# Linear attention and a GELU MLP on one core: loads in order of use, a reordered layer norm, masks between layer norms, x reloaded, z as a bf16 pair

## Chip, cores, metric

One core of one Trainium2 chip. The metric is the device time of one execution in microseconds (us). The changed kernel and the kernel before run on the same chip in turn, several times each. TensorE multiplies matrices into banks of its result memory, PSUM; VectorE, ScalarE and GpSimd work elementwise; each has its own queue of instructions, in program order. All runs compared below are of the fast state, or single looks (state unknown), which are called so. The span in the profile is just under 2 us shorter than the device time.

## The reference

```python
def _layernorm(x): return (x - mean(x)) / sqrt(var(x) + 1e-5)        # over the last axis
# attention, H = 32 heads of 20:
q, k, v = split(xn @ wqkv)
phi = lambda t: where(t > 0, t + 1, exp(t)) + 1e-6
kv  = einsum("bhsd,bhse->bhde", phi(k), v)
z   = einsum("bhsd->bhd", phi(k))
o   = einsum("bhqd,bhde->bhqe", phi(q), kv) / (einsum("bhqd,bhd->bhq", phi(q), z) + 1e-6)
A   = o @ wo
B   = gelu(xn @ w1 + b1) @ w2 + b2
out = x + A + B            # xn = _layernorm(x); x: 1 x 2048 x 640, F = 1536, all bf16
```

The kernel never forms v. It takes G = xnᵀ·phi(k), then KV from Wv and G, then M = KV·Wo, so that the attention's output is phi(q)/den · M, and it accumulates this in the same PSUM banks as the MLP's second product. S = 2048 gives 16 token tiles of 128.

## The kernel before

A small planner records instructions per engine in program order and puts in semaphore waits from declared reads and writes. TensorE's order is: warm-up fillers, MLP first product (with a transpose of the next tile between its units), K, G ("KV" below), Q chunk 0, z, KV, Q chunk 1, M, den, Q chunks 2 and 3, output tiles. The parts that the change touches (cuts marked; lines that are only comments sum up what is cut):

```python
        x_res = sb("x_res", [P, NT, D], BF16)          # x, kept for the residual
        xn_tm = sb("xn_tm", [P, NT, D], BF16)          # normalised x
        xnT = sb("xnT", [P, DT, S], BF16)              # its transpose
        PKQ = sb("PKQ", [P, NT * D], BF16)             # phi(k), later phi(q)
        # ... cut ...
        dma_x(0, 1)
        for i in range(NW1 - 1):
            dma_w1("scalar", i)                        # W1 quarters 0..2 in ScalarE's queue
        # b1, then
        dma_x(1, 1); dma_x(2, 2)
        dma_w1("sync", NW1 - 1)
        # x4..15, Wk, Wq, Wv, b2, Wo, W2 in SyncE's queue
        # ... cut ...
        def ln_stats(t):
            s = t % 4
            xt = x_res[:, t, :]
            Pl.ins(v, lambda e: e.bn_stats(stats[:, s, 0:6], xt[:, 0:HW]),
                   reads=[r_x[t]], writes=[r_stats[s]])
            ev = Pl.ins(v, lambda e: e.bn_stats(stats[:, s, 6:12], xt[:, HW:D]),
                        reads=[r_x[t]], writes=[r_stats[s]])
            Pl.ins(v, lambda e: e.bn_aggr(aggr[:, s, :], stats[:, s, :]),
                   reads=[r_stats[s]], writes=[r_aggr[s]])
            # ... cut: GpSimd computes rstd from aggr ...
        def ln_norm(t):
            s = t % 4
            Pl.ins(v, lambda e: e.tensor_scalar(xn_tm[:, t, :], x_res[:, t, :], aggr[:, s, 0:1], rstd[:, s:s + 1],
                                                ALU.subtract, ALU.mult),
                   reads=[r_x[t], r_aggr[s], r_rstd[s]], writes=[r_xn[t]])
        # ... cut: transp(t), five TensorE transposes, then VectorE's copy to xnT ...
        # ... cut ...
        filler(11)
        ln_stats(0)
        ln_stats(1)            # waits for x1 ...
        ln_norm(0)             # ... and this stands behind it
        b1_step()
        transp(0)
        filler(2)
        ln_stats(2)
        ln_norm(1)
        segs = [(0, 1), (1, 1), (2, 1), (3, 1), (4, 2), (6, 2), (8, 4), (12, 4)]
        for (t0, n) in segs:
            for jb in range(JT):                       # 12 units of 128 MLP columns
                while ...:                             # a next transpose is due
                    transp(nxt); ln_stats(nxt + 2); ln_norm(nxt + 1)
                h_unit(t0, n, jb)
        const_masks()                                  # GpSimd, after all layer norms
        # ... cut ...
        def phi(src, b, nb, dst, res_dst, extra_w):
            # ... cut: et, e2, d2, br; ek has three buffers ...
            Pl.ins("scalar", lambda e: e.activation(e2, src, ACT.Exp), reads=br, writes=[r_ek[s]])
            Pl.ins(v, lambda e: e.tensor_scalar(et, et, 1.0, 1e-6, ALU.min, ALU.add),      # "the min/add"
                   reads=[r_ek[s]], writes=[r_ek[s]])
            Pl.ins(v, lambda e: e.scalar_tensor_tensor(out=d2, in0=src, scalar=0.0, in1=e2,
                                                       op0=ALU.max, op1=ALU.add),
                   reads=br + [r_ek[s]], writes=[res_dst] + extra_w)
        # ... cut ...
        def z_step():
            b = take(1)
            Pl.ins("tensor", [(lambda e, j=j: e.matmul(bank(b, 2 * j, 2 * j + 1), zsum[:, j:D:DT], onesf[:],
                                                       start=True, stop=True)) for j in range(DT)],
                   reads=[r_zsum, r_small], writes=[B_[b]])
            # ... cut ...
        def den_step(c):
            # TensorE: den; VectorE: + 1e-6, reciprocal -> rden,
            # VectorE: five times PQ = PQ * rden       "the PQ multiplies"
        def xb(t):             # on GpSimd: "the additions"
            Pl.ins(g, lambda e: e.tensor_tensor(out=x_res[:, t, :], in0=x_res[:, t, :], in1=b2bc[:], op=ALU.add),
                   reads=[r_x[t], r_b2], writes=[r_x[t]])

        for t in range(NT):
            xb(t)              # as soon as GpSimd has finished the masks
        q_chunk(0); z_step(); kvt_step(); q_chunk(1); m_step(); den_step(0)
        q_chunk(2); q_chunk(3)
        # output tiles: 24 matmuls HG x W2 and 10 PQ x M into one bank pair,
        # VectorE: out_sb = PSUM + x_res, SyncE: store
```

Of the kernel before, what the change touches and what calls it, by code (L numbers as in the profile page):

```python
# [5 lines left out]
ALU = AluOpType  # L6
ACT = mybir.ActivationFunctionType
P = 128
# [104 lines left out]
def bass_parallel_sum__linear_attn_block__dense_activation_gelu__prompt_kernel(  # L113
# [23 lines left out]
    with contextlib.ExitStack() as es:  # L137
        sb = lambda *a, **k: es.enter_context(nc.sbuf_tensor(*a, **k))

        x_res = sb("x_res", [P, NT, D], BF16)  # L140
        xn_tm = sb("xn_tm", [P, NT, D], BF16)
        xnT = sb("xnT", [P, DT, S], BF16)
        PKQ = sb("PKQ", [P, NT * D], BF16)
        PK = PKQ[:].rearrange("p (t d) -> p t d", t=NT)
        PQ = PKQ[:].rearrange("p (j s) -> p j s", j=DT)
# [8 lines left out]
        Msb = sb("Msb", [P, DT, D], BF16)  # L154
# [7 lines left out]
        onesf = sb("onesf", [P, 1], FP32)  # L162
# [6 lines left out]
        zsum = sb("zsum", [P, D], FP32)  # L169
# [27 lines left out]
        r_x = [R_("x%d" % t) for t in range(NT)]  # L197
        r_xb = [R_("xb%d" % t) for t in range(NT)]
# [18 lines left out]
        r_zsum, r_z, r_ZB = R_("zsum"), R_("z"), R_("ZB")  # L217
# [6 lines left out]
        def dma_x(t, n):  # L224
            src = xv[t * P:(t + n) * P, :].rearrange("(t p) d -> p t d", p=P)
            Pl.ins("sync", lambda e: e.dma_start(x_res[:, t:t + n, :], src),
                   writes=r_x[t:t + n], dma=True)
# [6 lines left out]
        FW = F // NW1  # L234
        dma_x(0, 1)
        def dma_w1(eng, i):
            dma_w(eng, W1[:, :, i * FW:(i + 1) * FW], w1v[:, :, i * FW:(i + 1) * FW], r_W1[i])
        for i in range(NW1 - 1):
            dma_w1("scalar", i)
        dma_w("sync", b1tmp[:], B_b1.rearrange("(a p) -> a p", p=P), r_b1tmp)  # L240
        dma_x(1, 1)
        dma_x(2, 2)
        dma_w1("sync", NW1 - 1)
# [13 lines left out]
        Pl.ins(g, lambda e: e.memset(onesf[:], 1.0), writes=[r_small])  # L257
# [6 lines left out]
        def const_masks():  # L264
            def band(dst, res, base, n, step):
                Pl.ins(g, lambda e: e.memset(dst, 1.0), writes=[res])
                Pl.ins(g, lambda e: e.affine_select(
                    out=dst, in_=dst, compare_op=ALU.is_ge, fill=0.0,
                    base=base, pattern=[[-step, n], [0, step]], channel_multiplier=1),
                    reads=[res], writes=[res])  # L270
                Pl.ins(g, lambda e: e.affine_select(
                    out=dst, in_=dst, compare_op=ALU.is_ge, fill=0.0,
                    base=step - 1 - base, pattern=[[step, n], [0, step]], channel_multiplier=-1),
                    reads=[res], writes=[res])
            for t in range(DT):
                band(maskKV[t][:], r_masks, P * t - e0[t], Wd[t] // DH, DH)
            band(bmask[:], r_bmask, 0, H, 4)
# [15 lines left out]
        def ln_stats(t):  # L293
            s = t % 4
            xt = x_res[:, t, :]
            Pl.ins(v, lambda e: e.bn_stats(stats[:, s, 0:6], xt[:, 0:HW]),  # L296
                   reads=[r_x[t]], writes=[r_stats[s]])
            ev = Pl.ins(v, lambda e: e.bn_stats(stats[:, s, 6:12], xt[:, HW:D]),  # L298
                        reads=[r_x[t]], writes=[r_stats[s]])
            Pl.ins(v, lambda e: e.bn_aggr(aggr[:, s, :], stats[:, s, :]),  # L300
                   reads=[r_stats[s]], writes=[r_aggr[s]])
            Pl.ins(g, lambda e: e.tensor_single_scalar(veps[:, s:s + 1], aggr[:, s, 1:2], EPS, ALU.add),
                   reads=[r_aggr[s]], writes=[r_veps[s]])
            Pl.ins(g, lambda e: e.tensor_tensor(out=rstd[:, s:s + 1], in0=veps[:, s:s + 1],
                                                in1=mhalf[:], op=ALU.pow),
                   reads=[r_veps[s], r_small], writes=[r_rstd[s]])

        def ln_norm(t):
            s = t % 4
            Pl.ins(v, lambda e: e.tensor_scalar(xn_tm[:, t, :], x_res[:, t, :], aggr[:, s, 0:1], rstd[:, s:s + 1],  # L310
                                                ALU.subtract, ALU.mult),
                   reads=[r_x[t], r_aggr[s], r_rstd[s]], writes=[r_xn[t]])

        def transp(t):
            b = take(1)
            pT = bank(b).bitcast(BF16)[:, 0:D]
            Pl.ins("tensor", [(lambda e, k=k: e.transpose(pT[:, k * P:(k + 1) * P],  # L317
                                                          xn_tm[:, t, k * P:(k + 1) * P], ident[:]))
                              for k in range(DT)],
                   reads=[r_xn[t], r_ident], writes=[B_[b]])  # L320
            Pl.ins(v, lambda e: e.tensor_copy(xnT[:, :, t * P:(t + 1) * P],  # L321
                                              pT.rearrange("p (k q) -> p k q", k=DT)),
                   reads=[B_[b]], writes=[r_xnT[t]])
# [12 lines left out]

        filler(11)
        ln_stats(0)
        ln_stats(1)
        ln_norm(0)  # L340
        b1_step()
        transp(0)
        filler(2)
        ln_stats(2)
        ln_norm(1)
        segs = [(0, 1), (1, 1), (2, 1), (3, 1), (4, 2), (6, 2), (8, 4), (12, 4)]
        now, nxt = 0.0, 1
        for (t0, n) in segs:
            for jb in range(JT):
                while nxt < NT and (nxt < t0 + n or now >= 1.9 + 2.45 * (nxt - 1)):  # L350
                    transp(nxt)
                    if nxt + 2 < NT:
                        ln_stats(nxt + 2)
                    if nxt + 1 < NT:
                        ln_norm(nxt + 1)
                    nxt += 1
                    now += 0.3
                h_unit(t0, n, jb)
                now += 0.285 * n
        const_masks()  # L360
# [18 lines left out]
        for t in range(NT):  # L379
            b = take(2)  # L380
            fns = []
            for k in range(DT):
                for h in range(2):
                    fns.append(lambda e, k=k, h=h, b=b, t=t: e.matmul(  # L384
                        bank(b + h, 0, HW), xnT[:, k, t * P:(t + 1) * P],
                        Wqkv[:, k, D + h * HW:D + (h + 1) * HW], start=(k == 0), stop=(k == DT - 1)))
            Pl.ins("tensor", fns, reads=[r_xnT[t], r_Wk], writes=B_[b:b + 2])
            phi(pair(b), b, 2, PK[:, t, :], r_PK[t], [])
# [13 lines left out]
        Pl.ins(v, lambda e: e.tensor_tensor(out=zsum[:], in0=PK[:, 0, :], in1=PK[:, 1, :], op=ALU.add),  # L402
               reads=[r_PK[0], r_PK[1]], writes=[r_zsum])
        for t in range(2, NT):
            Pl.ins(v, lambda e, t=t: e.tensor_tensor(out=zsum[:], in0=zsum[:], in1=PK[:, t, :], op=ALU.add),  # L405
                   reads=[r_PK[t], r_zsum], writes=[r_zsum])


        def q_chunk(c):
            cc = slice(c * CW, (c + 1) * CW)  # L410
            for j in range(DT):
                b = take(1)
                Pl.ins("tensor", [(lambda e, k=k, j=j, b=b: e.matmul(  # L413
                    bank(b), Wqkv[:, k, j:D:DT], xnT[:, k, cc],
                    start=(k == 0), stop=(k == DT - 1))) for k in range(DT)],
                    reads=[r_Wq] + r_xnT[c * CH:(c + 1) * CH], writes=[B_[b]])
                phi(bank(b), b, 1, PQ[:, j, cc], r_PQ[c][j], r_PK)

        def z_step():
            b = take(1)  # L420
            Pl.ins("tensor", [(lambda e, j=j: e.matmul(bank(b, 2 * j, 2 * j + 1), zsum[:, j:D:DT], onesf[:],  # L421
                                                       start=True, stop=True)) for j in range(DT)],
                   reads=[r_zsum, r_small], writes=[B_[b]])
            Pl.ins(v, lambda e: e.tensor_copy(z_sb[:], bank(b, 0, 2 * DT)[:, 0:2 * DT:2]), reads=[B_[b]], writes=[r_z])
            for j in range(DT):
                Pl.ins(v, lambda e, j=j: e.tensor_scalar(ZB[:, j, :], bmask[:], z_sb[:, j:j + 1], None, ALU.mult),
                       reads=[r_z, r_bmask], writes=[r_ZB])
# [12 lines left out]
        def m_step():  # L440
            for j in range(DT):
                b = take(2)
                fns = []
                for t in range(DT):
                    for h in range(2):
# [5 lines left out]
                       reads=B_[b:b + 2], writes=[r_M[j]])  # L451
# [13 lines left out]

        def xb(t):
            Pl.ins(g, lambda e: e.tensor_tensor(out=x_res[:, t, :], in0=x_res[:, t, :], in1=b2bc[:], op=ALU.add),  # L467
                   reads=[r_x[t], r_b2], writes=[r_x[t]])

        for t in range(NT):  # L470
            xb(t)
# [7 lines left out]
        q_chunk(3)  # L479


        def out_tile(t):
# [12 lines left out]
            if not last:  # L495
                for i in range(n):
# [4 lines left out]
                       reads=B_[b:b + 2] + [r_x[t]], writes=[r_out[s]])  # L501
                Pl.ins("sync", lambda e: e.dma_start(ov[tok, :], out_sb[:, s, :]), reads=[r_out[s]], dma=True)
            else:
                for h in range(2):
# [5 lines left out]
                        reads=[B_[b + h], r_x[t]], writes=[r_out[h]])  # L510
# [47 lines left out]
```

## Time and profile before

| | |
|---|---|
| time, median of 3 runs | 229.88 us (229.44 to 230.40) |
| span in the profile | 228.1 us |
| TensorE (PE) busy | 218.6 us |
| first MLP matmul / first K matmul / first output matmul | 9.82 / 69.59 / 148.19 us |

The page of the kernel before, span and busy time by engine. PE busy is not PE at its peak, but it says that little is left outside TensorE's own work:

```profile
span 228.1 us, 3958 instructions
...
PE 218.6 (96%) x1634; PEld 151.4 (66%) x1643; DVE 122.8 (54%) x225; ACT 76.5 (34%) x146; POOL 42.0 (18%) x74
```

The waits view of the kernel before, TensorE only: who waited for whom, us in total, times, longest.

```profile
PE ps L317 <- DVE xn_tm L310: 3.0, 2, 2.5
PE ps L384 <- DVE PKQ L374: 1.5, 1, 1.5
PE ps L282 <- DVE warm L255: 1.3, 1, 1.3
PE ps L493 <- DVE PKQ L374: 0.3, 1, 0.3
```

Two waits matter: 2.5 us for the first normalised tile and 1.5 us at the start of K.

The head, in the timeline of the kernel before: start, duration, engine, instruction, in brackets the idle time before it and what ended it.

```profile
3.37 0.49 DVE L296 BATCH_NORM_STATS2 stats<-x_res 128x6 f32<-128x320 bf16 x1 [2.17 <-DMA x_res<-in_A_x_dram]
...
7.06 0.49 DVE L296 BATCH_NORM_STATS2 stats<-x_res 128x6 f32<-128x320 bf16 x1 [2.42 <-DMA x_res<-in_A_x_dram]
...
8.24 0.39 DVE L310 TENSOR_SCALAR xn_tm<-x_res,aggr,rstd 128x640 bf16<-128x640 bf16 x1
...
8.69 0.45 PE L317 MATMUL ps<-ident,xn_tm 128*128 128x128 bf16 x5 [2.53 <-DVE xn_tm L310]
...
9.82 3.45 PE L329 MATMUL ps<-xnT,W 128*128 128x128 bf16 x35
```

The statistics at 7.06 us are tile 1's, and they wait for a load. Tile 0's normalisation (8.24) stands behind them in VectorE's queue, although its rstd was ready at 5.6 us. TensorE idles meanwhile, and the 35 matmuls that follow are slow. The stretches view shows why (each row a stretch; the columns are busy time by engine, then the granted TensorE clock, DMA share and GB/s):

```profile
core 0: us, PE busy (x) PEld busy (x) DVE busy (x) ACT busy (x) POOL busy (x), PEclk, DMA share, GB/s
5.90:9.20 3.30, 0.77 (x9) 0.48 (x8) 1.53 (x5) 1.46 (x2) 0.71 (x2) 1.00 1.09 340
9.30:12.60 3.30, 3.25 (x29) 2.81 (x28) 1.78 (x5) 1.47 (x4) 0.94 (x3) 0.50 1.08 352
12.70:16.00 3.30, 3.30 (x62) 3.29 (x60) 1.91 (x5) 3.11 (x11) 0.58 (x2) 1.00 1.07 362
```

TensorE was busy for 0.77 us of the 3.3 us up to 9.2, and the next 3.3 us ran at half clock. The Trainium skill, "TensorE: Matmul & The Clock Gate", Part 1, describes this: free-running activity windows of about 3.4 us, after an idle one of which the clock is halved. This trace agrees, though the window was not quite idle: its clock records show half clock from 9.25 to 12.66 us, after a window (5.83 to 9.24 us) in which TensorE was busy for 0.88 us.

The start of K, timeline of the kernel before:

```profile
63.24 12.21 POOL L467 TENSOR_TENSOR x_res<-x_res,b2bc 128x640 bf16<-128x640 bf16 x9
...
72.53 3.10 DVE L372 TENSOR_SCALAR ek<-ek 128x640 bf16<-128x640 bf16 x1 [22.75 <-ACT ek L371]
...
75.74 0.82 DVE L374 SCALAR_TENSOR_TENSOR PKQ<-ps,ek 128x640 bf16<-128x640 f32 x1
76.48 0.32 DVE L372 TENSOR_SCALAR ek<-ek 128x640 bf16<-128x640 bf16 x1
...
76.71 5.46 PE L384 MATMUL ps<-Wqkv,xnT 128*128 128x320 bf16 x39 [1.52 <-DVE PKQ L374]
```

The first min/add takes 3.10 us, the second 0.32. The first one runs beside GpSimd's last additions and ends at 75.63 us, 0.2 us after them. TensorE waits for the bank for 1.52 us.

The z product, timeline of TensorE:

```profile
120.14 2.16 PE L421 MATMUL ps<-onesf,zsum 128*128 128x1 f32 x10
122.16 1.72 PE L432 MATMUL ps<-W,Wqkv 128*128 128x140 bf16 x25
```

### The profile page before, as it was taken

How to read it: one execution, taken by the hardware profiler on the slowest of the kernel's cores; microseconds unless marked ns; L12 is line 12 of the kernel's file. 1: busy time of each engine (PE TensorE's matmuls, PEld its weight loads, DVE VectorE, ACT ScalarE, POOL GpSimd, SP SyncE). 2: the span in 40 equal slices, each digit the busy share in tenths (PEclk: the TensorE clock that was granted, in tenths of full speed). 3: DMA queues.
4: the chain of work that ended last, by engine and by line, in shares of the span. 5: the costliest groups of instructions: out<-in, count | busy, mean ns of one | idle time of the engine just before them, and what ended most of it. 6: DMA issues, size and time to landing. Idle time of an engine off the chain costs nothing.

```text
span 228.1 us, 3958 instructions
## 1 busy us (share of the span) xinstructions
PE 218.6 (96%) x1634; PEld 151.4 (66%) x1643; DVE 122.8 (54%) x225; ACT 76.5 (34%) x146; POOL 42.0 (18%) x74
## 2 busy tenths in 40 slices
PE   7599999999999799999999999999999999999995
PEld 2399888544446477777758675467776776777773
DVE  2557777730002998899248809989316622911221
ACT  2388867556667355221152553420000000000000
POOL 2223333379999200000000000000000000000000
PEclk9889999999999999999999999999999999999999
DMA  6999930000000000000000000000110000010001
GB/s 205 342 363 363 363 129 0 0 3 1 0 0 3 0 0 3 0 0 3 0 0 3 1 0 0 0 3 29 50 39 29 29 32 32 25 60 29 29 32 57
DMA packets 11577, 12.87 MB, mean 56 GB/s; under 512 B 552, under 2 KB 11560, under 8 KB 11560
## 3 DMA queue, kind: packets, MB, share of 16 engines
q1 hardware_dynamic: 9592, 11.15, 14.4%
q10 hardware_dynamic: 1968, 1.47, 2.1%
q8 instruction: 13, 0.21, 0.4%
q14 instruction: 4, 0.03, 0.0%
HBM read 10.00 MB, written 2.62 MB: 55 GB/s over the span
## 4 chain that ended last, share of the span: by engine, by line
PE 83%; DVE 11%; DMA 2%; ACT 1%; issue 1%; SPq 0%; DVEq 0%
PE ps L493 32%; PE ps L329 20%; PE ps L395 10%; PE ps L384 7%; PE ps L413 5%; PE ps L446 3%; PE ps L317 3%; DMA x_res<-in_A_x_dram 2%; DVE PKQ L374 2%; PE ps L456 2%; DVE ek L372 2%; DVE rden L461 1%; DVE stats L298 1%; DVE stats L296 1%; PE ps L421 1%
## 5 line engine op out<-in xcount | busy, mean ns | idle before, releaser
L329 PE MATMUL ps<-xnT,W 128*128 128x128 bf16 (+2 forms) x477 | 56.2, 277 | 0.2
L493 PE MATMUL ps<-W,HG 128*128 128x320 bf16 x384 | 54.9, 299 | 0.3 <-DVE PKQ L374 0.3
L333 ACT ACTIVATE HG<-ps,b1c 128x128 bf16<-128x128 f32 (+2 forms) x96 | 42.3, 474 | 20.5 <-PE ps L329 19.2
L329 PEld LDWEIGHTS ps<-xnT,W 128*128 128x128 bf16 x480 | 38.0, 101 | 15.1 <-issue 0.7
L493 PEld LDWEIGHTS ps<-W,HG 128*128 128x128 bf16 x384 | 37.5, 98 | 15.7 <-issue 0.7
L499 DVE TENSOR_TENSOR out_sb<-ps,x_res 128x640 bf16<-128x640 f32 x15 | 12.3, 823 | 38.2 <-PE ps L493 38.2
L371 ACT ACTIVATE ek<-ps 128x512 bf16<-128x512 f32 (+1 forms) x36 | 23.2, 645 | 27.1 <-PE ps L384 8.7
L372 DVE TENSOR_SCALAR ek<-ek 128x512 bf16<-128x512 bf16 (+1 forms) x36 | 13.7, 379 | 30.4 <-ACT ek L371 29.8
L374 DVE SCALAR_TENSOR_TENSOR PKQ<-ps,ek 128x512 bf16<-128x512 f32 (+1 forms) x36 | 27.0, 751 | 3.8
L493 PE MATMUL ps<-Msb,PKQ 128*128 128x320 bf16 x160 | 24.5, 299 | 0.0
L384 PE MATMUL ps<-Wqkv,xnT 128*128 128x320 bf16 x160 | 22.1, 299 | 1.5 <-DVE PKQ L374 1.5
L395 PE MATMUL ps<-PKQ,xn_tm 128*128 128x320 bf16 x160 | 21.9, 299 | 0.0
L413 PE MATMUL ps<-xnT,Wqkv 128*128 128x512 bf16 x97 | 21.6, 379 | 0.2
L467 POOL TENSOR_TENSOR x_res<-x_res,b2bc 128x640 bf16<-128x640 bf16 x16 | 21.7, 1395 | 0.0
L384 PEld LDWEIGHTS ps<-Wqkv,xnT 128*128 128x128 bf16 x160 | 15.6, 98 | 8.0 <-issue 1.8
L493 PEld LDWEIGHTS ps<-Msb,PKQ 128*128 128x128 bf16 x160 | 15.7, 98 | 6.1
L395 PEld LDWEIGHTS ps<-PKQ,xn_tm 128*128 128x128 bf16 x160 | 15.7, 98 | 6.1
L413 PEld LDWEIGHTS ps<-xnT,Wqkv 128*128 128x128 bf16 x100 | 11.7, 117 | 9.6
L321 DVE COPY xnT<-ps 128x640 bf16<-128x640 bf16 x16 | 7.9, 491 | 12.1 <-PE ps L317 12.1
L461 DVE RECIPROCAL rden<-den_sb 128x512 bf16<-128x512 f32 x4 | 13.4, 3353 | 0.1
L405 DVE TENSOR_TENSOR zsum<-zsum,PKQ 128x640 f32<-128x640 f32 x14 | 11.5, 824 | 0.5
L317 PE MATMUL ps<-ident,xn_tm 128*128 128x128 bf16 x80 | 7.2, 221 | 3.3 <-DVE xn_tm L310 3.0
(48 smaller groups left out, 112.7 us busy)
## 6 DMA issues: line engine op xcount, KB each, us to landing
Wqkv<-in_A_wqkv_dram SPq DMA_DIRECT2D x3, 800.0 KB, 12.3
out_dram<-out_sb SPq DMA_DIRECT2D x15, 160.0 KB, 1.8
x_res<-in_A_x_dram SPq DMA_DIRECT2D x3, 640.0 KB, 10.7
W<-in_B_w_dram SPq DMA_DIRECT2D x1, 1920.0 KB, 15.6
W<-in_B_w_dram ACTq DMA_DIRECT2D x3, 480.0 KB, 5.7
Wo<-in_A_wo_dram SPq DMA_DIRECT2D x1, 800.0 KB, 10.7
W<-in_B_w_dram SPq DMA_DIRECT2D x1, 480.0 KB, 8.2
x_res<-in_A_x_dram SPq DMA_DIRECT2D x2, 160.0 KB, 3.9
```

The lines of the kernel that those rows point to most:

```text
L317: Pl.ins("tensor", [(lambda e, k=k: e.transpose(pT[:, k * P:(k + 1) * P], xn_tm[:, t, k * P:(k + 1) * P], ident[:])) for k in range(DT)], ...
L329: Pl.ins("tensor", [(lambda e, k=k: e.matmul(bank(b, 0, w), W1[:, k, jb * P:(jb + 1) * P], xnT[:, k, tok], start=(k == 0), stop=(k == DT - ...
L333: Pl.ins("scalar", lambda e: e.activation(HG[:, jb, tok], bank(b, 0, w), ACT.Gelu_apprx_tanh, bias=b1c[:, jb:jb + 1]), reads=[B_[b], r_b1c ...
L371: Pl.ins("scalar", lambda e: e.activation(e2, src, ACT.Exp), reads=br, writes=[r_ek[s]])
L372: Pl.ins(v, lambda e: e.tensor_scalar(et, et, 1.0, 1e-6, ALU.min, ALU.add), reads=[r_ek[s]], writes=[r_ek[s]])
L374: Pl.ins(v, lambda e: e.scalar_tensor_tensor(out=d2, in0=src, scalar=0.0, in1=e2, op0=ALU.max, op1=ALU.add), reads=br + [r_ek[s]], writes= ...
L384: fns.append(lambda e, k=k, h=h, b=b, t=t: e.matmul(bank(b + h, 0, HW), xnT[:, k, t * P:(t + 1) * P], Wqkv[:, k, D + h * HW:D + (h + 1) * ...
L395: Pl.ins("tensor", [(lambda e, t=t, h=h, b=b, f=f: e.matmul(bank(b + h, 0, HW), xn_tm[:, t, f * P:(f + 1) * P], PK[:, t, h * HW:(h + 1) * ...
L413: Pl.ins("tensor", [(lambda e, k=k, j=j, b=b: e.matmul(bank(b), Wqkv[:, k, j:D:DT], xnT[:, k, cc], start=(k == 0), stop=(k == DT - 1))) fo ...
L461: Pl.ins(v, lambda e: e.reciprocal(rden[:], den_sb[:]), reads=[r_den], writes=[r_rden])
L467: Pl.ins(g, lambda e: e.tensor_tensor(out=x_res[:, t, :], in0=x_res[:, t, :], in1=b2bc[:], op=ALU.add), reads=[r_x[t], r_b2], writes=[r_x[t]])
L493: return lambda e: e.matmul(bank(b + h, 0, HW), seq[i][0], seq[i][1][:, h * HW:(h + 1) * HW], start=(i == 0), stop=(i == n - 1))
```

## The change

Intent: let the first MLP units start earlier and without gaps (loads in one queue in order of use; tile 0 does not wait for tile 1; the MLP units of tiles 0 and 1 by quarters of W1), take GpSimd's additions away from the K start, and make z cheap. To have x for the residual after phi(k) has overwritten its tile, x is loaded a second time into the transposed tile once Q is finished. The diff, cut to its core:

```diff
-        x_res = sb("x_res", [P, NT, D], BF16)
+        xPK = sb("xPK", [P, NT, D], BF16)           # x, later phi(k)
+        x_in = xPK
+        PK = xPK
-        PKQ = sb("PKQ", [P, NT * D], BF16)
+        x_res = xnTf[:].rearrange("p (t d) -> p t d", t=NT)   # the tile of xnT
+        PQ = sb("PQ", [P, DT, S], BF16)
@@ loads @@
         dma_x(0, 1)
-        for i in range(NW1 - 1):
-            dma_w1("scalar", i)
         dma_w("sync", b1tmp[:], ...)
-        dma_x(1, 1)
-        dma_x(2, 2)
-        dma_w1("sync", NW1 - 1)
+        dma_w1(0)
+        dma_x(1, 1)
+        dma_w1(1)
+        dma_x(2, 1)
+        dma_w1(2)
+        dma_x(3, 1)
+        dma_w1(3)
@@ head @@
         ln_stats(0)
-        ln_stats(1)
         ln_norm(0)
+        tb = transp(0)
         b1_step()
-        transp(0)
-        filler(2)
-        ln_stats(2)
-        ln_norm(1)
+        filler(1)
+        ln_half(1, 0); xnT_copy(0, tb); ln_half(1, 1); ln_aggr(1)
+        ln_half(2, 0); ln_norm(1); ln_half(2, 1); ln_aggr(2)
@@ MLP loop, where a transpose is due @@
-                    transp(nxt)                     # with its copy
-                    ln_stats(nxt + 2)
-                    ln_norm(nxt + 1)
+                tb = transp(nxt)
+                ln_half(nxt + 2, 0)
+                xnT_copy(nxt, tb)
+                ln_norm(nxt + 1)
+                ln_half(nxt + 2, 1)
+                ln_aggr(nxt + 2)
+                run_masks(2)                        # two mask instructions on GpSimd
+        # plan: tile 0 units 0-5, tile 1 units 0-5, tiles 0+1 units 6-11, then as before
@@ z @@
+        zhl[0] = bf16(zsum); zhl[1] = bf16(zsum - zhl[0])
-        matmul(bank(b, 2*j, 2*j+1), zsum[:, j:D:DT], onesf)            # fp32, x5
+        matmul(bank(b, j, j+1), zhl[:, i, j:D:DT], onesb, start=(i == 0), stop=(i == 1))  # bf16, x10
@@ residual @@
-        for t in range(NT):
-            xb(t)
         q_chunk(0); ...; q_chunk(3)
+        for c in range(NC):
+            x_again(c)       # DMA of x into x_res; waits for all readers of xnT
+        for t in range(NT):
+            xb(t)
```

## The prediction

> **What bounds it now.** TensorE: busy 218.6 of 228.1 us, 83% of the chain that ended last. Its idle or slow places:
> - Head. The chain waits for x until 7.06 us, because VectorE takes tile 1's statistics (x landing 7.03 us, behind three W1 quarters on another queue) ahead of tile 0's normalisation. First MLP matmul 9.82 us; the next 35 take 3.45 us at a granted clock of 0.56 (the stretches view) against 2.0 us at full clock.
> - MLP: a tile's DVE chain (copy, two statistics, aggregate, normalise) plus transpose is 2.5 us, so every second transpose waits about 0.27 us, one 0.54: about 1.4 us in all.
> - Start of K: GpSimd's last b2 additions (16 x 1.35 us back to back, 53.8 to 75.4) overlap VectorE's first `min/add`, which takes 3.10 us instead of 0.32 and ends 0.2 us after GpSimd does; TensorE stalls 1.52 us.
> - z: ten fp32 weight loads of 0.31 us, 2.0 us.
>
> **What changes on the path.**
> - Head: normalisation of tile 0 no longer waits for x1; first MLP matmul at about 7.2 us. A new wait for tile 1 (about 1.4 us) gives part back; full clock comes earlier. Net -2 us. The reordered DVE work removes most of the 1.4 us MLP waits: -1.
> - The b2 additions leave the K start: -1.5.
> - z as ten bf16 loads (0.06 us spacing): -1.4. The extra copy and subtraction fall in 7 us of DVE idle time: 0.
> - Masks between layer norms: GpSimd has 1.5 us free per tile: 0.
> - Sum -5.7: last Q matmul at about 142 us instead of 147.8.
>
> **What comes back.** The reloads start only when the last Q matmul ends. 640 KB should land 3.2 to 3.6 us later (estimate: 160 KB stores land in 1.8 us, plus 480 KB at 363 GB/s; x0 plus the first W1 quarter took 3.5). Then 16 additions run back to back on GpSimd, 21.6 us. But VectorE still has its last phi tiles: before, the last `min/add` starts 4.2 us after the last Q matmul. It will find GpSimd busy. The Trainium skill, "SBUF — State Buffer", section "Who interferes with whom", says that a 2-port VectorE instruction and a GpSimd one exclude each other and that the later one fully blocks. This trace agrees, and shows more: the 3.10 us instruction got in at neither of two boundaries between GpSimd additions. So I expect VectorE starved for about 21 us (from 4 to 25 us after Q ends). The PSUM bank of the last Q tile is then needed by the third output tile, about 10.3 us after Q ends; TensorE idles about 16 us, then restarts at a low clock (about 2.5 us, estimate from the 1.4 us lost at the head).
>
> 229.9 - 5.7 + 15.6 + 2.5 = about 242; I shade to 240.
>
> **Prediction: 240 us, 80% range 223 to 246. Faster by over 2%: 0.26; within 2%: 0.12; slower: 0.62.**
>
> **What would show it.**
> - First MLP matmul near 7.2 us; K starts near 66.5 with no 3 us `min/add`; z near 0.6 us.
> - One VectorE `min/add` (or, if it slips ahead, a bf16 multiply of PQ by rden) lasting over 10 us beside the b2 additions, ending when GpSimd ends; a TensorE gap in the third output tile, and lower clock after it.
>
> **What would make it wrong.** If VectorE gets the port at a boundary between two additions, the loss is a microsecond or less: about 224. If the last `min/add` slips in ahead, only the PQ multiply (10 us after Q ends) is blocked: the fifth output tile waits about 4 us: about 228. If the addition hits the last but one `min/add`, the second output tile stalls: about 247. The head may give 1 or 4 us instead of 3.

## The result

| | before | after |
|---|---|---|
| median | 230.14 us (229.44 to 230.62, 4 runs) | 223.32 us (223.08 to 223.38, 4 runs) |
| span in the profile | 228.1 us | 221.4 us |

The ratio is 0.9704, 95% interval 0.9676 to 0.9732. Ratios here are the mean time of one kernel's fast runs over that of the other's in the same rounds, so not quite the ratio of the medians quoted.

The kernel is faster by 3%. The predicted 240 us is wrong, with the wrong sign. Where the 6.7 us of span come from is read from the starts of TensorE's stages in the two traces:

| stage | before | after | difference |
|---|---|---|---|
| start to first MLP matmul | 9.82 | 7.56 | -2.26 |
| MLP to first K matmul | 59.77 | 58.42 | -1.35 |
| K to first matmul of G | 23.42 | 21.74 | -1.68 |
| G and Q chunk 0 | 27.13 | 27.12 | 0 |
| z | 2.02 | 0.39 | -1.63 |
| KV to first output matmul | 26.03 | 26.04 | 0 |
| output tiles to the end | 79.91 | 80.13 | +0.2 |

The table is of one profile of each kernel. Two more profiles of the changed kernel (after_again, after_third) have the first MLP matmul at 7.44 and 7.06 us and the first K matmul at 66.22 and 65.86, so differences of a few tenths in these rows are no more than profiles of one kernel show.

The profile after, the lines that answer to those above. The page:

```profile
span 221.4 us, 3944 instructions
...
PE 214.4 (97%) x1603; PEld 148.6 (67%) x1612; DVE 125.8 (57%) x227; ACT 74.3 (34%) x140; POOL 41.7 (19%) x74
```

The waits of TensorE:

```profile
PE ps L350 <- DVE xnT L342: 1.9, 2, 1.3
PE ps L294 <- DVE warm L262: 1.2, 1, 1.2
PE ps L548 <- DVE PQ L417: 0.3, 1, 0.3
PE ps L334 <- DVE xn_tm L327: 0.2, 1, 0.2
```

The wait of 1.5 us at the K start is gone; a new one of 1.9 us (0.63 for the copy of tile 0, 1.29 for that of tile 1) is there; the second was predicted. The head in the timeline of the changed kernel:

```profile
5.42 0.45 DVE L327 TENSOR_SCALAR xn_tm<-xPK,aggr,rstd 128x640 bf16<-128x640 bf16 x1 [1.08 <-POOL rstd L316]
...
7.56 1.83 PE L350 MATMUL ps<-xnT,W 128*128 128x128 bf16 x30 [0.63 <-DVE xnT L342]
...
10.44 0.49 DVE L307 BATCH_NORM_STATS2 stats<-xPK 128x6 f32<-128x320 bf16 x1 [0.21 <-DMA xPK<-in_A_x_dram]
...
10.85 0.47 DVE L342 COPY xnT<-ps 128x640 bf16<-128x640 bf16 x1
...
11.38 2.39 PE L350 MATMUL ps<-xnT,W 128*128 128x128 bf16 x35 [1.29 <-DVE xnT L342]
```

Tile 0 is normalised at 5.42 instead of 8.24 us, and 30 matmuls take 1.83 us, at full clock. TensorE then waits 1.29 us for tile 1's copy, which stands behind a statistic of tile 3 that itself waited for a load (10.44).

The K start, and z:

```profile
65.98 6.28 PE L427 MATMUL ps<-Wqkv,xnT 128*128 128x320 bf16 x45
...
68.92 0.33 DVE L415 TENSOR_SCALAR ek<-ek 128x640 bf16<-128x640 bf16 x1 [23.83 <-ACT ek L414]
```

```profile
114.84 0.52 PE L468 MATMUL ps<-onesb,Msb 128*128 128x1 bf16 x10
115.23 1.72 PE L480 MATMUL ps<-W,Wqkv 128*128 128x140 bf16 x25
```

The first min/add takes 0.33 us. The start of the output stage, where the prediction put 16 us of idle time on TensorE:

```profile
141.29 13.34 SPq L516 DMA_DIRECT2D xnT<-in_A_x_dram  x4
...
145.02 0.28 DVE L415 TENSOR_SCALAR ek<-ek 128x512 bf16<-128x512 bf16 x1
145.35 22.60 POOL L520 TENSOR_TENSOR xnT<-xnT,b2bc 128x640 bf16<-128x640 bf16 x16 [102.12 <-DMA xnT<-in_A_x_dram]
...
151.69 6.88 DVE L511 TENSOR_TENSOR PQ<-PQ,rden 128x512 bf16<-128x512 bf16 x5
...
158.50 1.77 DVE L554 TENSOR_TENSOR out_sb<-ps,xnT 128x640 bf16<-128x640 f32 x2
...
164.08 1.52 PE L548 MATMUL ps<-Msb,PQ 128*128 128x320 bf16 x10
```

Two things are different from the prediction. The reload landed 4.06 us after it was issued, and it was issued 0.28 us after Q's end, so the additions began at 145.35 us; the last min/add had ended at 145.30. By chance they missed one another by 0.05 us. And the five PQ multiplies, which did meet the additions, were slowed but not shut out: 6.88 us instead of the 1.77 us of before. In the trace each of them ends about 0.3 us after the start of an addition, and the additions go on at 1.53 instead of 1.35 us. This will be called taking turns: VectorE gets in at the next boundary between two additions. The scaled PQ is first needed by the fifth output tile at 164.08 us, 5.5 us after the multiplies ended.

The near miss left the central claim of the prediction untested. Had the reload come a little earlier, would VectorE have been shut out for 20 us?

### The profile page after: what moved, and what is told of

The parts are those of the page before. It is cut to its first block, busy times and chain, and to the rows that moved or that the text cites. A ratio compares the mean times of both kernels' runs of the same rounds, so it can differ in the third digit from the quotient of the medians.

```text
span 221.4 us, 3944 instructions
## 1 busy us (share of the span) xinstructions
PE 214.4 (97%) x1603; PEld 148.6 (67%) x1612; DVE 125.8 (57%) x227; ACT 74.3 (34%) x140; POOL 41.7 (19%) x74
## 4 chain that ended last, share of the span: by engine, by line
PE 88%; DVE 5%; DMA 3%; SPq 1%; issue 1%; DVEq 0%
PE ps L548 33%; PE ps L350 23%; PE ps L438 10%; PE ps L427 10%; PE ps L460 5%; PE ps L494 3%; DMA xPK<-in_A_x_dram 3%; PE ps L504 2%; PE ps L334 2%; DVE PQ L417 2%; DVE rden L509 2%; DVE PQ L511 1%; SPq L235 1%; PE ps L480 1%; SPq L231 1%
## 5 line engine op out<-in xcount | busy, mean ns | idle before, releaser
L520 POOL TENSOR_TENSOR xnT<-xnT,b2bc 128x640 bf16<-128x640 bf16 x16 | 22.6, 1448 | 102.1 <-DMA xnT<-in_A_x_dram 102.1
L554 DVE TENSOR_TENSOR out_sb<-ps,xnT 128x640 bf16<-128x640 f32 x15 | 12.3, 823 | 33.4 <-PE ps L548 31.6
L548 PE MATMUL ps<-Msb,PQ 128*128 128x320 bf16 x160 | 24.5, 299 | 0.0
L438 PE MATMUL ps<-xPK,xn_tm 128*128 128x320 bf16 x160 | 21.9, 299 | 0.0
L548 PEld LDWEIGHTS ps<-Msb,PQ 128*128 128x128 bf16 x160 | 15.7, 98 | 6.1
L438 PEld LDWEIGHTS ps<-xPK,xn_tm 128*128 128x128 bf16 x160 | 15.7, 98 | 6.1
L307 DVE BATCH_NORM_STATS2 stats<-xPK 128x6 f32<-128x320 bf16 x32 | 15.1, 471 | 4.4 <-DMA xPK<-in_A_x_dram 4.4
L417 DVE SCALAR_TENSOR_TENSOR PQ<-ps,ek 128x512 bf16<-128x512 f32 x20 | 13.8, 692 | 2.1
L417 DVE SCALAR_TENSOR_TENSOR xPK<-ps,ek 128x640 bf16<-128x640 f32 x16 | 13.2, 825 | 1.7
L511 DVE TENSOR_TENSOR PQ<-PQ,rden 128x512 bf16<-128x512 bf16 x20 | 12.2, 674 | 0.1
```

Of the source, the lines that this page charges most:

```text
L307: Pl.ins(v, lambda e: e.bn_stats(stats[:, s, 6 * h:6 * h + 6], x_in[:, t, h * HW:(h + 1) * HW]), reads=[r_x[t]], writes=[r_stats[s]])
L438: Pl.ins("tensor", [(lambda e, t=t, h=h, b=b, f=f: e.matmul(bank(b + h, 0, HW), xn_tm[:, t, f * P:(f + 1) * P], PK[:, t, h * HW:(h + 1) * ...
L511: Pl.ins(v, lambda e, j=j: e.tensor_tensor(out=PQ[:, j, cc], in0=PQ[:, j, cc], in1=rden[:], op=ALU.mult), reads=[r_rden, r_PQ[c][j]], writ ...
L548: return lambda e: e.matmul(bank(b + h, 0, HW), seq[i][0], seq[i][1][:, h * HW:(h + 1) * HW], start=(i == 0), stop=(i == n - 1))
```

## Experiments

### Making the collision happen

**e1_collide.** The reload goes into the tile of the normalised x, which is free after G, and is released by Q chunk 2, so that it lands during the last phi tiles.

```diff
-        x_res = xnTf[:].rearrange("p (t d) -> p t d", t=NT)
+        x_res = xn_tm
-                   writes=[r_xr[c]] + r_xnT, dma=True)
+                   reads=[r_qmm[2]], writes=[r_xr[c]] + r_xn, dma=True)   # Q chunk 2 done
```

> The changed kernel, but x is reloaded into the tile of the normalised x (free since the KV product), and the reload is released by the last matmul of Q chunk 2, about 5.3 us earlier. So the b2 additions on GpSimd start near 140 us, while VectorE still has five or six min/add instructions of the phi tiles to do. Theory S (starvation, the prediction's): a min/add that finds GpSimd busy waits until the 16 additions end, so one lasts 15 us or more, TensorE stalls 15 to 20 us, about 240 us. Theory T (turns): each waiting VectorE instruction gets in at the next boundary between two additions, so each min/add lasts 0.3 to 1.7 us; VectorE falls behind by 3 to 6 us, TensorE stalls at most about 2 us: 223 to 226 us.

Measured: 223.86 us (223.62 to 223.98), ratio to before 0.9742 (0.9710 to 0.9774). Its timeline:

```profile
139.34 4.20 POOL L521 TENSOR_TENSOR xn_tm<-xn_tm,b2bc 128x640 bf16<-128x640 bf16 x3 [96.47 <-DMA xn_tm<-in_A_x_dram]
139.69 1.19 DVE L416 TENSOR_SCALAR ek<-ek 128x512 bf16<-128x512 bf16 x1
...
141.60 0.69 DVE L416 TENSOR_SCALAR ek<-ek 128x512 bf16<-128x512 bf16 x1
...
141.83 1.38 PE L549 MATMUL ps<-W,HG 128*128 128x320 bf16 x9 [1.17 <-DVE PQ L418]
```

Six min/adds met the additions, and each got in at the next boundary: 1.19 us for the first, 0.69 for the other five, instead of 0.28. Theory T (turns) holds and theory S (starvation) falls. The damage is one bank wait of 1.17 us instead of 0.26. The collision that the prediction feared costs about 0.4 us (223.47 us in e3_no_b2, without additions, on the same chip).

**e2_collide_tt.** As e1_collide, with the 512-wide min/add as a two-input minimum against a tile of ones.

```diff
-  tensor_scalar(et, et, 1.0, 1e-6, ALU.min, ALU.add)
+  tensor_tensor(out=et, in0=et, in1=warm[:], op=ALU.min)      # warm holds ones; Q tiles only
```

> As e1_collide, but the min/add on the 512-wide Q tiles is a two-input tensor_tensor minimum against a tile of ones (the 1e-6 is dropped, within tolerance). Theory S as refined by the result (a one-input 2-port instruction is starved, a two-input one takes turns as the PQ multiplies did, 1.53 us each): 223 to 227 us while e1_collide is near 240. Theory T: both within 1% of one another.

Measured: 224.44 us (224.35 to 224.96), within 0.3% of e1_collide. The six minima took 0.82 us each instead of 0.42. Both forms take turns; the form of the instruction does not decide.

**f1_add_in_k.** In the kernel before, the additions released by the third K tile, so that they meet the 640-wide min/adds of K, the very form that had waited 3.10 us.

```diff
-                   reads=[r_x[t], r_b2], writes=[r_x[t]])
+                   reads=[r_x[t], r_b2, r_gate], writes=[r_x[t]])
-            phi(pair(b), b, 2, PK[:, t, :], r_PK[t], [])
+            phi(pair(b), b, 2, PK[:, t, :], r_PK[t], [r_gate] if t == 2 else [])
```

> The kernel before, with the 16 b2 additions released by the third K tile, so that they run back to back from about 75 to 97 us, beside thirteen 640-wide min/add instructions, the very form that took 3.10 us in the profile of before. Theory S' (the 640-wide min/add in this stage is shut out until the additions end): one min/add of 15 us or more, TensorE idle over 12 us, 241 us or more. Theory T (turns, as in e1_collide): every min/add ends within about 0.2 us of a boundary between two additions (0.4 to 1.5 us each), VectorE keeps a pace of about 1.4 us per tile against TensorE's 1.36: K start stall of 1.5 us gone, 0 to 2 us lost, 228 to 230.5 us.

Measured: 228.10 us (227.34 to 228.90), ratio 0.9936 (0.9906 to 0.9966). Twelve min/adds met additions; they took 0.56 to 0.60 us. K took 21.73 us, as in the changed kernel (21.74). Turns again, and no wait on TensorE. One of the twelve:

```profile
77.92 0.59 DVE L373 TENSOR_SCALAR ek<-ek 128x640 bf16<-128x640 bf16 x1
```

**f2_add_late.** In the kernel before, the additions released by the last matmul of Q, without any reload (in this layout x is still in place): one part of the change alone.

```diff
         q_chunk(3)
+        for t in range(NT):
+            xb(t)            # reads r_gate, written by the matmuls of q_chunk(3)
```

> The kernel before, with the additions released by the last matmul of Q instead of running at the K start; no reload (x is still in place in this layout). Only that part of the change. If the 1.52 us stall at the K start is a pure loss on the path, 229.7 becomes 228.2 (-0.65%). The additions then start near 146.5, about 5 us before the last min/add: turns cost at most 1 us (228 to 229); starvation 15 us (245).

Measured: 228.28 us (226.53 to 228.67), ratio 0.9929 (0.9887 to 0.9970). The K stall is gone (K 21.73 us) and the four min/adds that met additions took 0.69 to 0.71 us. The gain is 1.3 us in the medians (0.7 to 2.6 us by the interval), which agrees with the wait of 1.5 us, and it does not need the reload; the reload is the price of another memory layout.

### Each part of the change

**e3_no_b2.** The changed kernel without the additions (b2 is left out of the result).

```diff
-        for t in range(NT):
-            xb(t)
-    reads=B_[b:b + 2] + [r_xb[t]], ...
+    reads=B_[b:b + 2] + [r_xr[t // CH]], ...
```

> The changed kernel with no b2 addition at all (b2 is about 0.0005 in size, so the result is off by that): the reload stays, GpSimd is idle in the output stage. If the PQ multiplies that take turns with GpSimd (6.9 us instead of 1.8) cost nothing, the time is that of the changed kernel, 223.3 +- 0.5; if the collision still costs something on the path, it is faster by up to 5 us.

Measured: 223.47 us (223.26 to 223.66). The PQ multiplies are back to 1.77 us and the time does not move: in the changed kernel the collision is wholly off the path.

**e4_z_fp32.** The changed kernel with z undone to five fp32 matmuls.

```diff
-   matmul(bank(b, j, j+1), zhl[:, i, j:D:DT], onesb, start=(i == 0), stop=(i == 1))
+   matmul(bank(b, 2*j, 2*j+1), zsum[:, j:D:DT], onesf, start=True, stop=True)
-   # the two VectorE instructions that split zsum
```

> The changed kernel with the z product undone to fp32 (five fp32 matmuls, no split). The trace says that ten bf16 passes saved 1.63 us (start to start 2.02 before, 0.39 after); if that is on the path, 223.3 becomes 224.9 (+0.7%). If the slack is eaten later by VectorE, +0.2 or less.

Measured: 224.84 us (224.60 to 225.04), 1.4 us above e3_no_b2 on the same chip and 1.5 above the changed kernel. z's own stretch is 2.0 us again. z is worth what it takes on TensorE.

**g1_old_loads.** The changed kernel with the loads as before (three W1 quarters in ScalarE's queue, x2 and x3 in one).

```diff
-   dma_w1(0); dma_x(1, 1); dma_w1(1); dma_x(2, 1); dma_w1(2); dma_x(3, 1); dma_w1(3)
+   for i in range(NW1 - 1): dma_w1("scalar", i)      # issued at once, beside x0
+   dma_x(1, 1); dma_x(2, 2); dma_w1("sync", NW1 - 1)
```

> The changed kernel with the loads issued as before (three W1 quarters in ScalarE's queue, x2 and x3 in one transfer), the new order of VectorE and of the MLP units kept. If the order of the loads is what counts in the head, x1 lands at about 7.0 instead of 6.5 and x2 and x3 later, and 1 to 3 us are lost (224.5 to 226.5); if the order of VectorE's work is what counts, under 0.7 us (223.3 to 224).

Measured: 223.38 us (223.21 to 223.49). The first MLP matmul starts at 8.02 instead of 7.56 us, but tile 1's units start at 11.49 instead of 11.38 and K at 66.09 instead of 65.98 (65.86 to 66.22 in the changed kernel's three profiles): what is lost first is waited for anyway at tile 1. The order of the loads, the first item in the change's name, is worth nothing measurable here.

**g2_old_dve_order.** The changed kernel with VectorE's order of before.

```diff
         ln_stats(0)
+        ln_stats(1)
         ln_norm(0)
@@ loop @@
-   ln_half(nxt + 2, 0); xnT_copy(nxt, tb); ln_norm(nxt + 1); ln_half(nxt + 2, 1); ln_aggr(nxt + 2)
+   xnT_copy(nxt, tb); ln_stats(nxt + 2); ln_norm(nxt + 1)
```

> The changed kernel with VectorE's order of before (both statistics of tile 1 ahead of tile 0's normalisation; in the loop the copy, both statistics, the aggregate, then the normalisation), loads and MLP plan as changed. If the order of VectorE's work makes the head's gain: first MLP matmul near 9.2 us instead of 7.56, waits of 0.3 us at every second transpose come back, +1.5 to 3 us: 224.8 to 226.3 us. If it does not matter: 223.3.

Measured: 226.85 us (226.02 to 227.19). In its trace the first MLP matmul is at 9.17 us, at half clock again, and K starts at 69.72, where the kernel before has 69.59 and the changed kernel 65.98:

```profile
9.17 3.28 PE L350 MATMUL ps<-xnT,W 128*128 128x128 bf16 x30 [0.24 <-DVE xnT L342]
...
69.72 0.57 PE L420 MATMUL ps<-Wqkv,xnT 128*128 128x320 bf16 x3
```

So without the new order of VectorE's work the whole gain of 3.6 us before K is lost, though the loads and the plan of the MLP units stay as changed. Whether the order gives it alone, with the old plan of units, was not run. (On this chip the changed kernel itself, below, ran at 223.43 to 225.56 and before at 227.57 to 229.52, so the times are less clear than the traces.)

### Why did one min/add wait over two boundaries?

Turns explain all runs so far except the line on which the prediction stood: in the profile of before, the min/add at 72.53 let the additions at 72.70 and 74.05 pass. Six runs looked for the reason.

**h1_shift_adds.** Three memsets ahead of the additions shift their phase.

```diff
+        for i in range(3):
+            memset(out_sb[:, 0, 0:P], 0.0)      # GpSimd
         for t in range(NT):
             xb(t)
```

> The kernel before, with three small memsets (0.2 to 0.3 us each) put before GpSimd's 16 additions, so that all additions run about 0.8 us later. The first min/add of K then asks for the port early inside an addition instead of 0.17 us before a boundary. If the double miss of before came from asking just before a boundary (theory P, phase), the min/add gets in at the first boundary, takes under 1.6 us, and the K stall shrinks to under 0.5 us: about 228.5 us. If the first min/add of K is shut out until GpSimd has run dry (theory S''), it takes about 3.9 us and the stall grows to about 2.3 us: about 230.5 us.

Measured: 231.91 us (230.13 to 232.05), ratio 1.0126 (1.0066 to 1.0187). The first min/add asked 0.5 us into an addition and still let two boundaries pass: 3.78 us, with a stall of 2.2 us. The phase is not the cause; in this run theory S'' is as good as right (3.9 and 2.3 us), and h2_more_adds tests it. This run has a second lesson: K took 25.77 us, 2.35 more than before, though its stall was only 0.7 us longer. The stretches view of h1_shift_adds, just after the stall:

```profile
77.00:80.30 3.30, 3.08 (x13) 1.81 (x14) 2.99 (x7) 1.04 (x2) 0.00 (x0) 0.56 0.00 0
```

The stall of 2.2 us was here followed by a stretch at a granted clock of 0.56. h2_more_adds, next, had 2.7 us of stall and no such stretch. The clock records of the two traces, which change at steps of 3.41 us, tell why. In h1_shift_adds the stall lies within one window (73.96 to 77.37 us), in which TensorE was busy for 1.21 us, and half clock follows. In h2_more_adds it is split between two (72.40 to 75.81 and 75.82 to 79.23), in which TensorE was busy for 1.91 and 2.19 us, and the clock stays full. Where a stall falls in the windows decides about this second cost.

**h2_more_adds.** Six more additions into a scratch tile after the 16.

```diff
+        for i in range(6):
+            tensor_tensor(out=out_sb[:, 0, :], in0=b2bc[:], in1=b2bc[:], op=ALU.add)   # GpSimd
```

> The kernel before, with six more additions of the same width (into a scratch tile) after the 16, so that GpSimd is busy until about 83.5 instead of 75.4 us. Theory S'' (shut out until GpSimd is idle): the first min/add of K takes about 11 us, TensorE stalls about 9.5 us, about 238 us. Turns with an occasional miss: the first min/add takes at most 3.1 us, the next ones 0.4 to 1.6 us, 229 to 231 us.

Measured: 228.14 us (227.94 to 230.13), the same as before (ratio 1.0006). Its timeline:

```profile
71.65 4.31 DVE L372 TENSOR_SCALAR ek<-ek 128x640 bf16<-128x640 bf16 x1 [22.75 <-ACT ek L371]
...
74.52 5.25 POOL L473 TENSOR_TENSOR out_sb<-b2bc 128x640 bf16<-128x640 bf16 x4
...
76.81 0.48 DVE L372 TENSOR_SCALAR ek<-ek 128x640 bf16<-128x640 bf16 x1
```

The min/add missed three boundaries (71.82, 73.17, 74.52) and got in at the fourth (75.85), with five of the six scratch additions still running or to come; the next ones took turns at 0.48 us. So even this one is not shut out until GpSimd is dry, and the first part of the expectation falls; but a miss of three is more than "at most 3.1 us" allowed. The test is weaker than planned: the scratch additions are not like the sixteen (they read one tile twice and took 1.25 instead of 1.40 us), and the min/add got in only behind the first of them.

**k1_probes** (one look). Five extra min/adds on scratch beside the additions, after idle time (A, C), at once (B) and after steady work (D, E).

```diff
+        probe([r_HG[12][0]])     # A: released by an MLP unit near 58 us
+        probe()                  # B
+        probe([r_HG[12][4]])     # C
+        busy(6); probe()         # D: after six half-tile statistics
+        busy(1); probe()         # E
```

> The kernel before, with five extra 640-wide min/add instructions on a scratch tile, in VectorE's idle time beside the additions: A after 8 us of idle time (near 58.6 us), B at once after A, C after 2 us or more of idle time (near 62.9), D after 3 us of steady statistics work, E after 0.5 us of it. If idle time before the request is what costs several boundaries: A and C take over 1.5 us (2 to 4 us), B, D and E under 1.6 us. If the place in GpSimd's stream decides (late additions), A to E all take turns (under 1.6 us) and the first min/add of K still takes about 3 us. No bearing on the time is claimed.

Measured: all five took turns at the first boundary, and so did the first min/add of K, which took 0.83 us; TensorE had no wait at the K start. Single time 227.76 us. The timeline, A and B together, and the first of K:

```profile
58.26 2.14 DVE L364 TENSOR_SCALAR out_sb<-out_sb 128x640 bf16<-128x640 bf16 x2 [8.26 <-ACT HG L333]
...
72.07 0.83 DVE L390 TENSOR_SCALAR ek<-ek 128x640 bf16<-128x640 bf16 x1 [3.31 <-ACT ek L389]
```

Neither idle time before the request (A) nor the place in GpSimd's stream (the first of K meets the 14th addition, as in before) makes it miss.

**k2_no_idle** (one look). VectorE kept busy with 42 statistics up to the first min/add of K.

```diff
+        for i in range(42):
+            bn_stats(stats[:, 0, 0:6], out_sb[:, 1, 0:HW])
```

> The kernel before, with 42 half-tile statistics on a scratch tile (0.52 us each) that keep VectorE busy from 50 to about 72 us, up to the first min/add of K. If idle time before the request is the cause, that min/add gets in at the first boundary (0.4 to 1.6 us instead of 3.1) and TensorE's stall at the K start goes below 0.5 us. If not, it takes about 3 us as before.

Measured: two misses again, 3.07 us, and a K stall of 1.5 us. So idle time is neither needed for a miss (here) nor enough for one (k1's A).

```profile
73.55 3.07 DVE L376 TENSOR_SCALAR ek<-ek 128x640 bf16<-128x640 bf16 x1
...
77.47 0.32 DVE L376 TENSOR_SCALAR ek<-ek 128x640 bf16<-128x640 bf16 x1
```

**k3_probe_mid** and **k4_probe_late** (one look each). A single extra min/add, in the 7th and in the 11th addition.

```diff
+        tensor_scalar(out_sb[:, 0, :], out_sb[:, 0, :], 1.0, 1e-6, ALU.min, ALU.add)
+             # reads r_HG[12][4] (k3) or r_HG[12][8] (k4)
```

> The kernel before, with one extra 640-wide min/add (released near 62.6 us, about six uncontended additions into the stretch). Theory Q (misses grow with the number of uncontended additions before the request; a turn resets it): the probe takes a turn or misses one boundary, and the first min/add of K, about six additions later, likewise: under 2.7 us, not 3.1, and the stall at the K start falls under 1 us. If the count does not matter, the first min/add of K takes about 3 us again.

> As k3_probe_mid with the probe near 66.9 us, about ten uncontended additions into the stretch. Theory Q: this probe misses more boundaries than that of k3_probe_mid (at least one, taking 1.5 to 5 us), and the first min/add of K, about two additions after it, takes a turn (under 1.6 us), so TensorE does not stall at the K start. If the count does not matter: the probe takes a turn and the first min/add of K misses.

Measured: k3's extra min/add took its turn (0.46 us), and so did the first of K (0.52 us). k4's took its turn too, at the first boundary, after 10 additions without a request (1.52 us; it had asked just after an addition began), and the first of K took 0.48 us. Neither has a stall at the K start. The growth with the number of additions that was expected is not there up to ten.

What the records give together:

| run | VectorE's request falls in addition no. | additions since the last turn | boundaries missed |
|---|---|---|---|
| e1_collide, f1_add_in_k, f2_add_late | 1 | 0 | 0 |
| k1_probes, A | 4 | 3 | 0 |
| changed kernel, first PQ multiply | 5 | 4 | 0 |
| k3_probe_mid, probe | 7 | 6 | 0 |
| k4_probe_late, probe | 11 | 10 | 0 |
| k1, k3, k4: first min/add of K | 14 | 2 to 6 | 0 |
| before, h1_shift_adds, k2_no_idle: first of K | 14 | 13 | 2 (then no more additions) |
| h2_more_adds: first of K | 14 | 13 | 3 |

In these profiles no request after an earlier turn in the same row of additions missed, and all four after thirteen additions without one did. Whether a threshold lies between ten and thirteen, and what builds up, is open; no run here shows it. Two limits:

- One execution of each kernel was profiled. The profiled one of h2_more_adds took 230.13 us; its other three took 227.94 to 228.18 at the same granted clock (0.993 and 0.992), as if they had no stall of 2.7 us. On that chip five of seven runs of the kernel before took 227.57 to 228.35 us at 0.992, against 229.80 in its profiled run on another chip. So the misses may come in some executions only, and the gain at the K start with them; this is not shown.
- In before, h1 and k2 the min/add got in only when the sixteen additions were over. Whether a longer row of the same additions would have kept it out longer was not run.

### A better version

**f3_fill_head.** Two more edits in the head of the changed kernel, aimed at the new 1.29 us wait.

```diff
-        for q in range(2): plan += [(0, 1, jb) ...]      # tile 0: units 0-5
-        for q in range(2): plan += [(1, 1, jb) ...]      # tile 1: units 0-5
-        plan += [(0, 2, jb) for jb in range(2 * JQ, JT)]
+        for t in range(2):
+            plan += [(t, 1, jb) for jb in range(3 * JQ)] # units 0-8 of each
+        plan += [(0, 2, jb) for jb in range(3 * JQ, JT)]
+                if nxt == 1:                              # tile 1's copy before tile 3's statistic
+                    xnT_copy(nxt, tb); ln_half(nxt + 2, 0)
```

> The changed kernel with two further edits in the head: the first nine MLP units of tile 0 instead of six run before tile 1's (they fill TensorE's wait for tile 1), and the copy of tile 1's transpose comes before tile 3's first statistics, which wait for a load. The first unit of tile 1 should start near 10.95 instead of 11.38 us with 45 instead of 30 matmuls done: -1.2 us, 222.1 us. If loads of W1's third quarter come later than 9.9 us, less.

Measured: 222.27 us (222.15 to 222.56), ratio to before 0.9683 (0.9663 to 0.9703).

**after_again.** The changed kernel on another chip (that of h1, h2 and g2).

> The changed kernel itself, unedited, on the same chip as the others, to compare: 223.3 us, and a spread of its runs under 0.5 us (that of before is 1 to 2 us).

Measured: 223.43, 223.52, 225.13 and 225.56 us, ratio 0.9823 (0.9766 to 0.9880): on this chip a gain of 2% is not shown. The expectation of a spread under 0.5 us fails. The list of runs tells where to look: the granted clock was 1.000 in the two short runs and 0.992 in the two long ones, which is what one half-clock window of 3.4 us makes (1.7 us lost). Neither long run was profiled, so where it fell is not shown. All runs of the kernel before whose clock is listed, but one, were at 0.985 to 0.993: part of the lead of the changed kernel is that it mostly has no such window. Because of the spread the comparison was repeated on one chip with five rounds:

**f3_again** and **after_third**, the two kernels unedited.

> f3_fill_head again, beside the changed kernel on one chip: its ratio to before is 0.4 to 0.6% below that of the changed kernel (222.2 against 223.3 us).

> The changed kernel, unedited: 223.3 us (0.970 of before), and each run of f3_again below each of its runs of the same state.

Measured: f3_again 222.46 us (221.74 to 222.68), ratio 0.9667 (0.9639 to 0.9695); the changed kernel 223.39 us (222.90 to 224.00), ratio 0.9722 (0.9694 to 0.9750). Every run of f3_again is below every run of the changed kernel. K starts at 64.46 against 65.86 us. The gain of 0.9 us is somewhat less than the 1.2 expected; the version beats both kernels.

## Why the prediction was wrong

Point by point:

- **The head, "Net -2", and "-1" for the MLP waits.** Right in sum: -3.6 us up to K, against -3. The table cuts otherwise than the prediction: its -2.26 is the start alone (7.56 us, predicted 7.2), and its -1.35 holds the wait for tile 1 (predicted 1.4 us, measured 1.29), the clock and the MLP waits. g2_old_dve_order shows that the gain needs VectorE's new order, g1_old_loads that it does not need the loads' new order.
- **The K start, "-1.5".** Right: -1.68 us in the trace; alone (f2_add_late) about 1.3 us in the medians.
- **z, "-1.4".** Right, a little low: -1.63 us; e4_z_fp32 gives 1.4 to 1.5.
- **Masks, "0", and the z split, "0".** Consistent with the traces: no wait of TensorE comes from them. They were not undone alone.
- **Sum "-5.7".** It was -6.9 us up to the first output matmul (148.19 to 141.27).
- **The failed step: "So I expect VectorE starved for about 21 us (from 4 to 25 us after Q ends)".** It added 18 us that did not exist, so that a gain was forecast as a loss. It failed twice over.
  - Its timing: "640 KB should land 3.2 to 3.6 us later". The reload landed 4.34 us after Q's end, and the additions came 0.05 us too late to meet the last min/add, which was luck. The estimate added bytes at full rate to the latency of a small store. In the stretches view the four microseconds after the issue moved 0, 137, 374 and 145 GB/s: nothing for one microsecond, and full rate only in one of four.
  - Its rule. "Got in at neither of two boundaries" was true of one instruction and was made a law. Where the collision was forced at the start of a row of additions, as the prediction's own case has it (e1_collide, f1_add_in_k, f2_add_late), every min/add got in at the next boundary. Turns cost up to one addition each (about 1.4 us), and the output stage has 5.5 us of slack for them (e3_no_b2: no difference without any additions).
- **"the fifth output tile waits about 4 us"**, the prediction's milder case for a min/add that slips ahead. It did slip ahead, and this failed for the same reason: the PQ multiplies took 6.88 us, not about 15, and nobody waited. The case named "If VectorE gets the port at a boundary ... about 224" is the one that came.
- **The chances.** 0.62 for slower rested on the one line; the right outcome had 0.26.

On the Trainium skill: "SBUF — State Buffer", section "Who interferes with whom", says that the second of the two engines to issue is blocked until the first finishes. Read as one instruction against one instruction, it agrees with every turn seen here: 0.69 us for a min/add that needs 0.28 alone. The prediction stretched it to a whole row of instructions, which the page does not say. It also says that a two-input instruction with both inputs in SBUF contends and one with a single SBUF input outside the 2-port modes does not; the trace agrees (four of five PQ multiplies 1.61 us instead of 0.42 beside additions; the output add, with one input in PSUM, 0.82 us both beside them and not).

## What to carry to other kernels

Look at which instruction stands in front of a ready one on an in-order engine before reordering loads: a statistic that waited for a load held back a normalisation whose inputs were there. Half of the gain was lost when VectorE's old order came back, nothing when the old order of the loads did. A single long instruction in a trace is one event, not a rule; before a forecast adds it up sixteen-fold, find a second one, or give the cheap reading (one instruction's length per collision) the larger chance. When two engines share a port, ask how much slack stands behind the slowed instruction: here 5 us of slower multiplies cost nothing.

## What the Trainium skill lacked or had wrong

- "SBUF — State Buffer", "Who interferes with whom": it does not say what happens against a row of back-to-back GpSimd instructions. In the profiles here VectorE got in at the next boundary in all collisions but four: after 13 additions without a turn a min/add missed two boundaries (3.07 to 3.78 us) or three (4.31 us). The cause is open.
- The same section has no figure for what such turns cost GpSimd, instruction by instruction. The additions went from 1.35 to 1.40 us apart beside 512-wide min/adds and to 1.53 beside PQ multiplies.
- "TensorE: Matmul & The Clock Gate", Part 1, does not say how much work in a window still counts as idle. In the profiles here, from the first clock record on, each window at full clock with at most 1.39 us of TensorE work in 3.41 us was followed by half clock (0.88 in before, 1.21 in h1_shift_adds, 1.39 in g2_old_dve_order), and each with at least 1.53 us by full clock (1.53 in e3_no_b2, 1.91 in h2_more_adds). Busy time is as the profile models it.
